# Laying k and v of five batches out the way q is laid out, and moving one transpose forward in the opening, in a fused linear-attention and SwiGLU kernel

## The chip, the cores and the metric

The kernel runs on one core of a Trainium2 chip. The metric is the device time of one execution in microseconds (us); lower is better. Every kernel is timed several times beside the unchanged kernel on the same chip. One early execution of the unchanged kernel took 857.58 us for no reason that was found. A profile is one execution recorded instruction by instruction. Its span is some 1.8 us shorter than the device time of the same execution (324.8 against 326.62 us for the kernel before), so spans are compared with spans and times with times.

The engines are called as in the profile: PE is the matrix engine (TensorE), PEld its weight loads, DVE the vector engine, ACT the scalar engine, POOL the GpSimd engine, SP the engine that issues most DMAs.

## The reference, cut to what matters

```python
# q, k, v: (8 batches, 8 heads, 576 tokens, 64) float32
theta = pi/2 * arange(576) / 576
phi(x) = concat([relu(x)*cos(theta), relu(x)*sin(theta)], axis=-1)   # 128 features
q_p, k_p = phi(q), phi(k)
kv  = einsum('bhsf,bhsd->bhfd', k_p, v)          # 128 x 64 per head, a sum over all 576 tokens
z   = sum(k_p, axis=2)
num = einsum('bhsf,bhfd->bhsd', q_p, kv)
den = einsum('bhsf,bhf->bhs', q_p, z) + 1e-6
x   = (num/den) as (4608 tokens, 512)
xn  = x / sqrt(mean(x*x) + 1e-6) * rms_g
out = (silu(xn @ w_gate) * (xn @ w_val)) @ w_out     # 512 -> 1536 -> 512, float32 out
```

The part that the change touches is kv and z. The kernel appends a column of ones to v (so E = 65 columns), and one matmul chain per head then gives kv and z together. This is called the kvz stage below: one for each batch, eight in all, and the change alters those of batches 3 to 7.

## The kernel before

Most of the time goes to the feed-forward part: blocks of 512 tokens, with 128x512 matmuls back to back. The attention of batch `nb` is slipped between the matmuls of block `nb-1`. 576 tokens are not a multiple of 128, so k and v are loaded with 9 tokens to a partition: two heads (2 x 576 tokens = 128 x 9) share the 128 partitions, the even head in rows 0 to 63 and the odd one in rows 64 to 127. So each matmul of the kvz stage uses 64 of the 128 rows, and it takes 8 heads x 9 = 72 of them.

```python
    def load_kv(which, b, r0=0, r1=4, j0=0, j1=NJ):          # NJ = 9
        ...  # raw tile [P, 4 pairs of heads, 9*64]
        return nc.sync.dma_start(
            out=raw[key][:, r0:r1, j0 * D : j1 * D],
            in_=src[b, 2 * r0 : 2 * r1, :, :].rearrange("h s d -> (h s d)")
            .rearrange("(r p n) -> p r n", p=P, n=NJ * D)[:, :, j0 * D : j1 * D],
        )

    def k_phi(eng, b, j, part, rs=(0, 4)):                    # one of the 9 tokens, cos or sin
        ...
        phi(eng, kp_main[b][:, j, rs[0] : rs[1], o],
            raw[("k", b)][:, rs[0] : rs[1], j * D : (j + 1) * D], f(5 + j))

    def kvz_mm(b, banks, rs=(0, 4)):
        for r in range(*rs):
            for j in range(NJ):
                for c in range(2):
                    lo = 64 * c
                    nc.tensor.matmul(
                        banks[c][:, r * E : (r + 1) * E],
                        lhsT=kp_main[b][lo : lo + 64, j, r, :],
                        rhs=vvm[b % 2][lo : lo + 64, r, j, :],
                        start=(j == 0), stop=(j == NJ - 1),
                    )
    # ... cut: q, whose tiles hold 4 tokens of a head to a partition (512 tokens, all 128 rows);
    # the last 64 tokens of heads 0-3 and 4-7 share a fifth tile (rows 0-63 and 64-127)

    # the opening, batch 0 (cut)
    q_tr_evac(A, 0, 2, psO[0][:, :])
    q_phi(A, 0, 3, 1)
    ...
    nd_pe(0, 2, psA)                    # products of q tile 2 with kvz
    nd_post(0, 2, psA)
    q_tr_pe(0, 3, psO[1][:, :])         # transposes of q tile 3
    q_tr_evac(A, 0, 3, psO[1][:, :])
    ...
    # loads of batches 3..7 run two batches ahead, one piece after each step of a block
```

Of the kernel before, what the change touches and what calls it, by code (L numbers as in the profile page):

```python
# [9 lines left out]
FP32 = mybir.dt.float32  # L10
BF16 = mybir.dt.bfloat16
AF = mybir.ActivationFunctionType
ALU = mybir.AluOpType
SYNC_DEP = mybir.DependencyInfo(mybir.DependencyClass.Sync, mybir.DependencyReason.DATA)



# [6 lines left out]
def kernel(  # L24
# [11 lines left out]
    nc = tc.nc  # L36
    B, H, S, D = q.shape
    DM = H * D
# [32 lines left out]
    def load_kv(which, b, r0=0, r1=4, j0=0, j1=NJ):  # L71

        key = (which, b)
        if key not in raw:
            raw[key] = (two if which == "k" else one).tile(
                [P, 4, NJ * D], FP32, name=f"r{which}", tag=f"r{which}"
            )
        src = {"k": k, "v": v}[which]
        return nc.sync.dma_start(
            out=raw[key][:, r0:r1, j0 * D : j1 * D],  # L80
            in_=src[b, 2 * r0 : 2 * r1, :, :]
            .rearrange("h s d -> (h s d)")
            .rearrange("(r p n) -> p r n", p=P, n=NJ * D)[:, :, j0 * D : j1 * D],
        )
# [10 lines left out]
    def load_q_tail(b):  # L95
# [6 lines left out]
            )  # L102
        return d

    def load_piece(which, b, p):
        if which != "q":
            load_kv(which, b, p, p + 1)
        elif p < 4:
            load_q(b, 2 * p, 2 * p + 2)
        else:  # L110
            load_q_tail(b)
# [68 lines left out]
    wg = one.tile([P, NDT, DFF], BF16, name="wg")  # L180
    wv = one.tile([P, NDT, DFF], BF16, name="wv")
    wo = one.tile([P, NNT, DM], BF16, name="wo")
    vvm = [one.tile([P, 4, NJ, E], BF16, name=f"vvm{i}") for i in range(2)]
    xnt_tail = one.tile([P, NDT, TB], BF16, name="xnt_tail")
    NXT = 5
    xts = [one.tile([P, DM + 4], FP32, name=f"xt{i}") for i in range(NXT)]
    for i in range(2):
        nc.gpsimd.memset(vvm[i][:, :, :, D:E], 1.0)
    eps_col = math.sqrt(DM * 1e-6)
    for i in range(NXT):  # L190
        nc.gpsimd.memset(xts[i][:, DM : DM + 1], eps_col)
# [16 lines left out]
    def phi(eng, out_ap, in_ap, scale):  # L208
        if eng is nc.scalar:
            nc.scalar.activation(out=out_ap, in_=in_ap, func=AF.Relu, scale=scale)  # L210
        else:
            eng.tensor_scalar(  # L212
                out=out_ap, in0=in_ap, scalar1=scale, scalar2=0.0, op0=ALU.mult, op1=ALU.max
            )

    def k_phi(eng, b, j, part, rs=(0, 4)):

        o = slice(0, D) if part == 0 else slice(D, F)
        f = cos_of if part == 0 else sin_of
        if b not in kp_main:  # L220
            kp_main[b] = one.tile([P, NJ, 4, F], BF16, name="kpm", tag="kpm")
        phi(
            eng, kp_main[b][:, j, rs[0] : rs[1], o],
            raw[("k", b)][:, rs[0] : rs[1], j * D : (j + 1) * D], f(5 + j),
        )

    def q_phi(eng, b, c, part):
        o = slice(0, D) if part == 0 else slice(D, F)
        f = cos_of if part == 0 else sin_of
        if (b, c) not in qp_tiles:  # L230
            qp_tiles[(b, c)] = four.tile(
                [P, H if c < 4 else 4, F], BF16, name="qp", tag="qp" if c < 4 else "qpt"
            )
        src = view4(raw[("q", b)], c) if c < 4 else raw[("qt", b)][:, :, :]
        phi(eng, qp_tiles[(b, c)][:, :, o], src, f(c))
# [15 lines left out]
    def q_tr_pe(b, c, bank):  # L251
        t = qp_tiles[(b, c)]
        dst = bank.bitcast(BF16).rearrange("p (h s) -> p h s", s=P)
        for h in range(H if c < 4 else 4):
            nc.tensor.transpose(dst[:, h, :], t[:, h, :], ident[:, :])  # L255

    def q_tr_evac(eng, b, c, bank, heads=(0, 8)):
        h0, h1 = heads if c < 4 else (0, 4)
        dst = bank.bitcast(BF16).rearrange("p (h s) -> p h s", s=P)
        copy(eng, q_dst(b, c)[:, h0:h1, :], dst[:, h0:h1, :])  # L260

    def copy(eng, o, i):
        if eng is nc.scalar:
            nc.scalar.copy(out=o, in_=i)  # L264
        else:
            eng.tensor_copy(out=o, in_=i)  # L266

    def v_cast(eng, b, r0=0, r1=4, j0=0, j1=NJ):
        copy(
            eng, vvm[b % 2][:, r0:r1, j0:j1, 0:D],  # L270
            raw[("v", b)][:, r0:r1, j0 * D : j1 * D].rearrange("p r (j d) -> p r j d", d=D),
        )

    def headview(pst):
        return pst[:, :, 0 : 4 * E].rearrange("p b (h e) -> p b h e", e=E)
# [29 lines left out]
    def nd_pe(b, j, pst):  # L305

        o = headview(pst)
        for h in range(H):
            g, i = h // 4, h % 4
            if j < 4:  # L310
                nc.tensor.matmul(  # L311
                    o[:, g, i, :], lhsT=qpT[(b, 0)][:, h, j * P : (j + 1) * P],
                    rhs=kvz_of(b, h), start=True, stop=True,
                )
            else:
                for bb in (b - 1, b):
                    lo = 64 * (bb % 2)
                    nc.tensor.matmul(
                        o[lo : lo + 64, g, i, :],
                        lhsT=qpT[(bb, 1)][:, i, 64 * g : 64 * g + 64],  # L320
                        rhs=kvz_of(bb, h), start=True, stop=True,
                    )
# [59 lines left out]
        rs_of[(b, j)] = rs  # L382

    xn_of = {}
    xg = one.tile([P, DM], FP32, name="xg")

    def x_gain(b, j, g):

# [41 lines left out]
    def x_tr_evac(eng, b, j, bank, part=(0, 4)):  # L430
        dst = bank.bitcast(BF16).rearrange("p (t s) -> p t s", s=P)
        copy(eng, x_dst(b, j)[:, part[0] : part[1], :], dst[:, part[0] : part[1], :])
# [167 lines left out]
    for half, (eng, bank) in enumerate(((A, psG[1]), (V, psV[1]))):  # L600
        part = (2 * half, 2 * half + 2)
        x_tr_pe(0, 0, bank[:, :], part)
        x_tr_evac(eng, 0, 0, bank[:, :], part)
    q_tr_evac(A, 0, 2, psO[0][:, :])
    q_phi(A, 0, 3, 1)
    x_norm(0, 1)
    q_phi(V, 0, 3, 0)
    open_ffn(0, (0, 1), 0, 128)
    x_tr_pe(0, 1, psV[1][:, :])
    x_tr_evac(V, 0, 1, psV[1][:, :])  # L610
    nd_pe(0, 2, psA)
    nd_post(0, 2, psA)
    q_tr_pe(0, 3, psO[1][:, :])
    q_tr_evac(A, 0, 3, psO[1][:, :])
    x_sq(0, 2)
    wo_load(0)
# [40 lines left out]
    def at(blk, n, where, f, *args):  # L657
        slots.setdefault((blk, n), none())[where].append((f, args))
# [26 lines left out]
    for nb in range(2, B):  # L685
        b = nb - 1
        late = nb == 2
        vb, vn = (b, 3) if late else (b - 1, 14)
        if nb == 3:
            vb, vn = b, 1  # L690
        if late:
            at(vb, vn, "post", v_cast, V, nb, *LOW)
        for j in range(NJ):
            kb, kn = (b, 1 + j // 7) if late else (b - 1, 12 + j // 3)
            if not late or j > 3:
                at(kb, kn, "post", k_phi, V, nb, j, 0)
            if not late or j > 1:
                at(kb, kn, "post", k_phi, A, nb, j, 1)
        for c in range(5):
            qn = (2, 3, 5, 5, 6)[c] if late else c  # L700
            at(b, qn, "post", q_phi, V, nb, c, 0)
            at(b, qn, "post", q_phi, A, nb, c, 1)
            at(b, qn, "post", q_tr_dma, nb, c)
        if not late:
            at(vb, vn, "post", v_cast, V, nb, *LOW)
        at(vb, vn + 1, "post", v_cast, V, nb, *HIGH)
        kz, nds = (6, (7, 9, 11, 12)) if late else (4, (5, 7, 9, 11))
        at(b, kz, "pe", kvz_pe, nb, psA)
        at(b, kz, "pre", kvz_evac, A, nb, psA, 0)
        at(b, kz, "pre", kvz_evac, A, nb, psA, 1)  # L710
        for j in range(4):
            n = nds[j]
            at(b, n, "mid" if n == NNT else "pe", nd_pe, nb, j, psA)
            at(b, n, "pre", nd_post, nb, j, psA)
            at(b, n, "post", x_sq, nb, j)
            where = "pre" if n + 1 >= NNT else "post"
            at(b, n + 1, where, x_norm, nb, j)
            at(b, n + 1, where, x_tr_dma, nb, j)
        if nb % 2 == 1:
            at(b, 13, "pe", nd_pe, nb, 4, psA)  # L720
            at(b, 13, "pre", nd_post, nb, 4, psA)
            at(b, 13, "post", x_sq, nb, 4)
            at(b, 14, "post", x_norm, nb, 4)
            at(b, 14, "post", x_tr_dma, nb, 4)
    for nb in range(3, B):

        b = nb - 2
        for i, which in enumerate(("k", "v", "q")):
            if (which, nb) == ("v", 3):
                at(b, 13, "post", load_kv, "v", nb, *LOW)  # L730
                at(b, 14, "post", load_kv, "v", nb, *HIGH)
                continue
            for p in range(5 if which == "q" else 4):
                n = (0, None, 6)[i] + p if b == 1 else 5 * i + p
                at(b + n // 16, n % 16, "post", load_piece, which, nb, p)

# [157 lines left out]
```

## Time and profile before

| what | value |
|---|---|
| time, median of 3 | 327.7 us (327.57, 327.7 and the one of 857.58, which is counted) |
| profiled execution | 326.62 us, span 324.8 us |
| PE busy | 316.5 us, 97% |
| matmuls of 512 columns, start to start | 216 ns |
| the five kvz stages, from the start of the matmul ahead to that of the one after | 1.58 us each |

Lines of the profile's page, kernel before: the span, busy time of each engine, the clock granted to PE in 40 slices (9 is 90% or more), the DMA packets, and the chain of waits that ended last by engine.

```profile
span 324.8 us, 6415 instructions
PE 316.5 (97%) x2409; PEld 161.8 (50%) x2444; DVE 186.0 (57%) x414; ACT 176.8 (54%) x367; POOL 31.9 (10%) x67
...
PEclk9999999999999999999999999999999999999999
...
DMA packets 80321, 53.91 MB, mean 166 GB/s; under 512 B 51361, under 2 KB 67745, under 8 KB 80290
...
PE 91%; ACT 4%; DVE 2%; issue 1%; DMA 1%; DVEq 0%; ACTq 0%
```

PE is the limit: it is busy nearly always and is 91% of the chain. Work taken from DVE or ACT is worth nothing unless PE waited for it.

One kvz stage in the timeline of PE, kernel before. The columns are start (us), duration (us), engine, line, operation, output and inputs, rows and columns, count:

```profile
96.17 1.03 PE L442 MATMUL psV<-xnT,wv 128*128 128x512 bf16 x4
97.13 1.33 PE L283 MATMUL psA<-vvm,kpm 64*128 64x65 bf16 x72
98.40 1.04 PE L442 MATMUL psG<-xnT,wg 128*128 128x512 bf16 x3
```

The same stage in the timeline of the weight loads, kernel before; in brackets stands the idle time ahead:

```profile
97.13 1.21 PEld L283 LDWEIGHTS <-kpm 64*128 64x128 bf16 x72 [0.42 <-issue]
```

Read the starts. Four matmuls of 512 columns begin at 96.17; the fourth should begin 3 x 216 ns later, at 96.82, and the next one 216 ns after that, at 97.03. The kvz stage begins at 97.13 instead. Its 72 matmuls run to 98.40, where the feed-forward goes on. In the start records behind these lines the last 512-column matmul takes 312 ns to the next start (96 more than its 216), and the last of the 72 takes 122 ns, where about 17 is usual for this form (105 more). The weight loads show the same edge: ahead of the first there is 0.42 us without a weight load, put down to nothing that the profile shows. So a stage costs 96 + 1143 + 122 = 1361 ns.

The groups of DVE and ACT that the change alters, kernel before (columns: line, engine, operation, output<-inputs, shapes, count | busy us, mean ns of one | idle before):

```profile
L210 ACT ACTIVATE kpm<-rk,tab 128x256 bf16<-128x256 f32 x63 | 27.4, 499 | 0.0
...
L212 DVE TENSOR_SCALAR kpm<-rk,tab 128x256 bf16<-128x256 f32 x63 | 18.1, 348 | 0.0
...
L311 PE MATMUL psA<-kvzs,qpT 128*128 128x65 bf16 x248 | 12.8, 194 | 0.3
...
L266 DVE CAST vvm<-rv 128x1152 bf16<-128x1152 f32 x13 | 9.5, 754 | 0.0
```

The PE line is not altered. It is the existing matmul of the form that the new kvz stage will have, 128 rows and 65 columns: eight of them start within 213 ns, so one every 30.5 ns. (The 194 ns is the latency of one, which overlaps with the next.)

The last lines that matter are those of the end: the last piece of the chain of waits, and then the closing instructions of SP (count, then min/median/max duration in ns, first and last start).

```profile
321.14 0.37 ACT osb L264
```

```profile
L889 SPq EVENT_SEMAPHORE  x11: 17/28/28, 322.1 to 324.8; - x11
...
L889 SPq DRAIN  x3: 7/7/13, 324.0 to 324.3; - x3
```

### The profile page before, as it was taken

Reading aid. Unit: us, or ns where it says so; the run is one execution under the profiler, and the core shown is the slowest. Engines: PE = TensorE matmul, PEld = TensorE weight load, DVE = VectorE, ACT = ScalarE, POOL = GpSimd, SP = SyncE. Lnnn points to the kernel's source line nnn. Section 1 sums busy time; section 2 is a strip of 40 time slices with the busy share of each in tenths; the row PEclk is TensorE's granted clock in tenths of the full one; section 3 lists DMA queues with packets and bytes.
Section 4 is the critical chain, followed back from the end, with each engine's and each line's share of the span. In section 5 each row is a group of like instructions: output and inputs, shape, how many; then the busy total and the mean of one; then the engine's idle time right before and its main releaser. Section 6 shows DMA issues by size and latency. Waiting matters only on the chain.

```text
span 324.8 us, 6415 instructions
## 1 busy us (share of the span) xinstructions
PE 316.5 (97%) x2409; PEld 161.8 (50%) x2444; DVE 186.0 (57%) x414; ACT 176.8 (54%) x367; POOL 31.9 (10%) x67
## 2 busy tenths in 40 slices
PE   8899999999999999999999999999999999999995
PEld 2587465554445444544454445444544444444443
DVE  6975768777766765578257745773577133203410
ACT  6973865965774467546664475456644233223321
POOL 1660202001100110010001100110011000000000
PEclk9999999999999999999999999999999999999999
DMA  7999999797599576976597679956611400020014
GB/s 258 274 199 251 313 200 337 270 193 195 141 276 265 159 195 164 211 195 192 160 212 211 165 195 218 199 151 214 126 39 32 131 32 0 26 105 1 0 34 97
DMA packets 80321, 53.91 MB, mean 166 GB/s; under 512 B 51361, under 2 KB 67745, under 8 KB 80290
## 3 DMA queue, kind: packets, MB, share of 16 engines
q1 hardware_dynamic: 73248, 48.64, 57.6%
q0 software_dynamic: 6880, 4.72, 9.9%
q8 instruction: 19, 0.31, 0.4%
q10 hardware_dynamic: 162, 0.13, 0.2%
q14 instruction: 12, 0.10, 0.1%
HBM read 37.75 MB, written 9.44 MB: 145 GB/s over the span
## 4 chain that ended last, share of the span: by engine, by line
PE 91%; ACT 4%; DVE 2%; issue 1%; DMA 1%; DVEq 0%; ACTq 0%
PE psC L462 26%; PE psG L442 26%; PE psV L442 26%; PE psA L283 3%; PE psA L311 2%; ACT kpm L210 2%; PE psG L462 2%; PE psG L581 1%; DMA rk<-in_k_dram 1%; PE psV L581 1%; PE psO L581 1%; PE psV L255 1%; ACT qp L210 1%; PE psO L255 1%; ACT sg L451 0%
## 5 line engine op out<-in xcount | busy, mean ns | idle before, releaser
L457 DVE TENSOR_TENSOR hT<-psV,sg 128x512 bf16<-128x512 f32 x102 | 70.3, 689 | 93.9 <-PE psV L442 70.1
L451 ACT ACTIVATE sg<-psG 128x512 f32<-128x512 f32 x102 | 60.6, 594 | 65.1 <-PE psG L442 63.9
L442 PE MATMUL psV<-xnT,wv 128*128 128x512 bf16 (+1 forms) x365 | 92.1, 374 | 0.4
L442 PE MATMUL psG<-xnT,wg 128*128 128x512 bf16 (+1 forms) x352 | 90.9, 374 | 0.7
L462 PE MATMUL psC<-wo,hT 128*128 128x512 bf16 x382 | 88.2, 379 | 0.7
L442 PEld LDWEIGHTS <-wv 128*128 128x128 bf16 x416 | 40.7, 98 | 47.4
L462 PEld LDWEIGHTS <-hT 128*128 128x128 bf16 x420 | 40.2, 98 | 46.7
L442 PEld LDWEIGHTS <-wg 128*128 128x128 bf16 x416 | 38.5, 98 | 41.0 <-DVE xnT L266 0.4
L264 ACT COPY osb<-psC 128x512 f32<-128x512 f32 (+1 forms) x33 | 19.1, 578 | 39.7 <-PE psC L462 39.0
L381 POOL TENSOR_TENSOR rs<-ms,mhalf 128x1 f32<-128x1 f32 x36 | 19.8, 549 | 199.8 <-ACT scr L376 199.8
L403 DVE SCALAR_TENSOR_TENSOR xn<-xt,rs,gb 128x512 bf16<-128x512 f32 x35 | 26.1, 745 | 16.6 <-POOL rs L381 16.6
L376 ACT ACTIVATE scr<-xt 128x513 bf16<-128x513 f32 x36 | 22.8, 635 | 22.8 <-DVE xt L365 22.6
L210 ACT ACTIVATE kpm<-rk,tab 128x256 bf16<-128x256 f32 (+1 forms) x78 | 31.9, 477 | 1.6 <-DMA rk<-in_k_dram 1.6
L365 DVE TENSOR_TENSOR xt<-psA,rec 128x512 f32<-128x512 f32 x35 | 24.2, 691 | 1.2
L212 DVE TENSOR_SCALAR kpm<-rk,tab 128x256 bf16<-128x256 f32 (+1 forms) x84 | 22.3, 330 | 2.1 <-DMA rk<-in_k_dram 2.1
L210 ACT ACTIVATE qp<-rq,tab 128x512 bf16<-128x512 f32 x32 | 22.4, 714 | 0.0
L212 DVE TENSOR_SCALAR qp<-rq,tab 128x512 bf16<-128x512 f32 x32 | 15.1, 485 | 0.0
L311 PEld LDWEIGHTS <-qpT 128*128 128x128 bf16 x248 | 11.6, 98 | 6.7 <-issue 0.3
L311 PE MATMUL psA<-kvzs,qpT 128*128 128x65 bf16 x248 | 12.8, 194 | 0.3
L442 PE MATMUL psG<-xnt_tail,wg 128*128 128x512 bf16 x48 | 12.3, 379 | 0.1
L442 PE MATMUL psV<-xnt_tail,wv 128*128 128x512 bf16 x47 | 12.1, 379 | 0.0
L283 PEld LDWEIGHTS <-kpm 64*128 64x128 bf16 x576 | 9.9, 94 | 3.5 <-issue 2.7
(91 smaller groups left out, 170.3 us busy)
## 6 DMA issues: line engine op xcount, KB each, us to landing
out_dram<-osb SPq DMA_DIRECT2D x32, 256.0 KB, 2.8
rk<-in_k_dram SPq DMA_DIRECT2D x21, 288.0 KB, 4.6
rq<-in_q_dram SPq DMA_DIRECT2D x20, 256.0 KB, 3.1
rv<-in_v_dram SPq DMA_DIRECT2D x17, 288.0 KB, 3.2
rv<-in_v_dram SPq DMA_DIRECT2D x5, 576.0 KB, 7.7
rq<-in_q_dram SPq DMA_DIRECT2D x2, 1024.0 KB, 8.7
wo<-in_moe_w_out_dram POOLq DMA_DIRECT2D x4, 384.0 KB, 6.9
rk<-in_k_dram SPq DMA_DIRECT2D x2, 576.0 KB, 4.1
```

The source lines that it names most:

```text
L210: nc.scalar.activation(out=out_ap, in_=in_ap, func=AF.Relu, scale=scale)
L212: eng.tensor_scalar(out=out_ap, in0=in_ap, scalar1=scale, scalar2=0.0, op0=ALU.mult, op1=ALU.max)
L283: nc.tensor.matmul(banks[c][:, r * E : (r + 1) * E], lhsT=kp_main[b][lo : lo + 64, j, r, :], rhs=vvm[b % 2][lo : lo + 64, r, j, :], start= ...
L311: nc.tensor.matmul(o[:, g, i, :], lhsT=qpT[(b, 0)][:, h, j * P : (j + 1) * P], rhs=kvz_of(b, h), start=True, stop=True,)
L365: nc.vector.tensor_tensor(out=xt[:, 0:DM].rearrange("p (b h d) -> p b h d", b=2, d=D), in0=o[:, :, :, 0:D], in1=rec[:, :, :].unsqueeze(3). ...
L376: nc.scalar.activation(out=scr[:, :], in_=xt[:, 0 : DM + 1], func=AF.Square, scale=1.0 / math.sqrt(DM), accum_out=ms[:, :],)
L381: nc.gpsimd.tensor_tensor(out=rs[:, :], in0=ms[:, :], in1=mhalf[:, :], op=ALU.pow)
L403: nc.vector.scalar_tensor_tensor(out=xn[:, :], in0=x_of[(b, j)][:, 0:DM], scalar=rs_of[(b, j)][:, :], in1=gb[:, :], op0=ALU.mult, op1=ALU. ...
L442: nc.tensor.matmul(pst[bank][:, cols[0] : cols[1]], lhsT=w[:, t, n * P : (n + 1) * P], rhs=x[:, t, cols[0] : cols[1]], start=(t == 0), sto ...
L451: nc.scalar.activation(out=sg[:, :], in_=psG[bank][:, :], func=AF.Silu)
L457: nc.vector.tensor_tensor(out=hTs[blk][:, n, :], in0=psV[bank][:, :], in1=sg[:, :], op=ALU.mult)
L462: nc.tensor.matmul(bank, lhsT=hTs[blk][:, n, j * P : (j + 1) * P], rhs=wo[:, n, :], start=(n == 0), stop=(n == NNT - 1),)
```

## The change

Its intent: k and v of batches 3 to 7 take q's layout. A partition holds 4 tokens of every head, so 512 tokens fill all 128 rows and give 4 matmuls per head. The last 64 tokens of heads 0 to 3 lie in rows 0 to 63 of a fifth tile, those of heads 4 to 7 in rows 64 to 127. The fifth matmul of a head uses all 128 rows too, against a v tile `vvt` that is zero in the other heads' rows, so it stays in the same mode of the array. A stage has 40 matmuls in place of 72, and five wide phi operations for each of cos and sin in place of nine narrow ones. In the opening, q tile 3 is transposed ahead of tile 2's products.

```diff
+    def load_heads(which, b, h0, h1):
+        nc.sync.dma_start(
+            out=kv_tile(which, b)[:, h0 * 4 * D : h1 * 4 * D].rearrange("p (h n) -> p h n", n=4 * D),
+            in_=src[b, h0:h1, 0:512, :].rearrange("h (p j) d -> p h (j d)", j=4))
+    def load_last(which, b):                     # two DMAs: heads 0-3, heads 4-7
+        for g in range(2):
+            nc.sync.dma_start(
+                out=kv_tile(which, b)[64 * g : 64 * g + 64, 2048:2304]...,
+                in_=src[b, 4 * g : 4 * g + 4, 512:576, :].rearrange("h s d -> s h d"))
...
+    vvt = [one.tile([P, H, E], BF16, name=f"vvt{i}") for i in range(2)]
     for i in range(2):
         nc.gpsimd.memset(vvm[i][:, :, :, D:E], 1.0)
+        nc.gpsimd.memset(vvt[i][64:128, 0:4, :], 0.0)
+        nc.gpsimd.memset(vvt[i][0:64, 4:8, :], 0.0)
+        nc.gpsimd.memset(vvt[i][0:64, 0:4, D:E], 1.0)
+        nc.gpsimd.memset(vvt[i][64:128, 4:8, D:E], 1.0)
...   (k_phi_as_q: 5 operations of 512, the fifth of 256; v_cast_as_q on DVE;
...    v_cast_last: two casts of 64x256 on POOL)
+    def kvz_as_q(b, pst):
+        for h in range(H):
+            for c in range(5):
+                nc.tensor.matmul(
+                    pst[:, h % 2, h // 2 * E : (h // 2 + 1) * E],
+                    lhsT=kp_of(b)[:, 8 * c + (h if c < 4 else h % 4), :],
+                    rhs=vv_of(b)[:, c, h, :] if c < 4 else vvt[b % 2][:, h, :],
+                    start=(c == 0), stop=(c == 4))
...   (a scratch tile shares the buffers of another, to make room for vvt)
+    q_phi(A, 0, 3, 1)
     q_tr_evac(A, 0, 2, psO[0][:, :])
-    q_phi(A, 0, 3, 1)
...
+    q_tr_pe(0, 3, psO[1][:, :])
     nd_pe(0, 2, psA)
     nd_post(0, 2, psA)
-    q_tr_pe(0, 3, psO[1][:, :])
...
-        at(b, kz, "pe", kvz_pe, nb, psA)
+        at(b, kz, "pe", kvz_pe if late else kvz_as_q, nb, psA)       # late: batch 2
...
-            for p in range(5 if which == "q" else 4):
+            for p in range(5):                                       # 6 DMAs for k, 6 for v
```

## The prediction

> **What bounds the kernel.** TensorE. PE is busy 316.5 of 324.8 us (97%, page), granted clock 1.00 (DVE 57%, ACT 54%, POOL 10%); the chain of waits is 91% PE. In order of time, full matmuls (128x512) start every 216 ns nearly without holes from 30 us on. A block is 33.4 to 33.9 us: 144 of them (31.1 us), its products with kvz, one kvz stage. So only PE time or a new PE wait counts.
>
> **PE, the five kvz stages of batches 3 to 7.** Before: 72 matmuls with 64 rows, in pairs, 1143 ns from first to last start. The last 512-column matmul ahead of them takes 312 ns to the next start (216 is normal), the last of the 72 122 ns (17 is normal). The Trainium skill, "TensorEngine Tiling (Array Packing)", Key Properties, says that changing the tiling mode drains TensorE; these 96 and 105 ns agree. In all 96+1143+122 = 1361 ns. After: 40 matmuls of 128x128 weights and 65 columns, no change of mode. The products with kvz have the same form and start every 30.5 ns (213 ns over 7), so 40 x 30.5 = 1220 ns. Gain 0.14 us a stage, 0.7 us in all, on the chain.
>
> **DVE and ACT.** k of a batch: nine operations of 256 elements (348 ns on DVE, 499 on ACT) become four of 512 (485 and 714, as q's) and one of 256: -0.85 us DVE, -1.14 us ACT a batch. v's casts: 1152 to 1024 elements, 754 to some 680 ns. About -5 us on each engine, off the chain: worth nothing.
>
> **POOL.** Eight memsets at the start (free: weight loads wait 8.1 us there anyway) and two casts of 64x256 a batch, estimated 0.4 to 0.7 us each from the 0.55 us of one-element work in the trace.
>
> **DMA.** k and v of a batch go from 512 runs of 2304 B each to 1024 of 1 KB and 512 of 256 B: some 10,000 more packets, and 20 more issues of about 0.6 us on SP. DMA is 60 to 70% busy and loads come early, so this is hidden, but for v of batch 3. Before, its second half landed at 95.6 us and kvz started at 97.1. Now its last tokens land later (estimate 96 to 96.5), then come two POOL casts in turn; kvz needs the first at its fifth matmul. I expect one PE wait of 0 to 0.6 us, some 0.2.
>
> **Opening.** Before, PE waits 0.18 us for q tile 3's phi after tile 2's products. Now the transposes go first, but the products wait for an eviction that ACT does after the phi (0.74+1.02 us, to about 18.9). PE waits as long elsewhere. Worth 0, at most 0.1 either way.
>
> **Sum.** 327.7 - 0.7 + 0.2 + 0.0 = 327.2 us; range 326.3 to 328.2. Faster by over 2%: 0.01; within 2%: 0.97; slower: 0.02.
>
> **What would show it.** Right: the five kvz stages show 40 matmuls about 30 ns apart, no 312 and 122 ns at their edges, blocks of batches 4 to 7 shorter by about 0.14 us; DVE about 181 us, ACT about 171; the opening ends as before. Wrong: kvz matmuls further apart than 30 ns, a PE wait on POOL's vvt longer than 0.6 us or in more than one block, q transposes of batch 3 (2 us of slack) late behind SP's extra issues. Another risk: k or v of later blocks late, a us or more each.

## The result, and the profile after

The changed kernel takes 327.03 us (median of 6, 326.72 to 327.26), the kernel before 327.5 us beside it. The ratio of the two is 0.999, with a 95% interval of 0.9976 to 1.0004: the same, by a threshold of 2%. Ratios here are the mean time of one kernel's fast runs over that of the other's of the same rounds, so they are not quite the ratio of the medians. The difference of those means is 0.33 us (327.36 to 327.03). Executions over 1.5% slower than the fastest of the same kernel are left out of the means.

The same lines of the page, kernel after:

```profile
span 325.4 us, 6119 instructions
PE 316.4 (97%) x2249; PEld 162.6 (50%) x2284; DVE 183.9 (57%) x394; ACT 173.4 (53%) x347; POOL 38.9 (12%) x85
...
PEclk9999999999999999999999999999999999999999
...
DMA packets 90881, 53.90 MB, mean 166 GB/s; under 512 B 56801, under 2 KB 83425, under 8 KB 90850
...
PE 90%; DMA 3%; ACT 2%; DVE 2%; issue 1%; SPq 0%; DVEq 0%
```

The span is longer by 0.6 us although the times are shorter. One profiled execution is one draw: the start of this one happened to be late, as is shown below. So the two traces are compared part by part, not by their totals.

The kvz stage in the timeline of PE, kernel after:

```profile
97.05 1.03 PE L524 MATMUL psV<-xnT,wv 128*128 128x512 bf16 x4
97.91 0.29 PE L349 MATMUL psA<-vvm,kpm 128*128 128x65 bf16 x4
98.03 0.19 PE L349 MATMUL psA<-vvt,kpm 128*128 128x65 bf16 x1
98.06 0.29 PE L349 MATMUL psA<-vvm,kpm 128*128 128x65 bf16 x4
...
99.10 0.20 PE L349 MATMUL psA<-vvt,kpm 128*128 128x65 bf16 x1
99.13 0.81 PE L524 MATMUL psG<-xnT,wg 128*128 128x512 bf16 x2
```

Its weight loads, kernel after:

```profile
97.70 1.47 PEld L349 LDWEIGHTS <-kpm 128*128 128x128 bf16 x40
```

Both edges are gone. The first kvz matmul starts at 97.91, four times 216 ns after 97.05, and the feed-forward goes on 0.03 us after the last kvz matmul. The weight loads begin 0.2 us ahead of their matmuls, with no idle time noted: they overlap with the matmuls before, which they did not across the old edge. In the start records: 216 ns in, 1183 to 1185 ns from first to last start, 34 or 35 ns out, so 1219 ns where the prediction said 1220.

The groups of DVE, ACT and POOL, kernel after:

```profile
L247 ACT ACTIVATE kpm<-rk,tab 128x512 bf16<-128x512 f32 x20 | 13.3, 714 | 0.0
...
L249 DVE TENSOR_SCALAR kpm<-rk,tab 128x512 bf16<-128x512 f32 x20 | 8.9, 492 | 0.0
...
L318 DVE CAST vvm<-rv 128x1024 bf16<-128x1024 f32 x10 | 6.5, 681 | 0.0
...
L318 POOL CAST vvt<-rv 64x256 bf16<-64x256 f32 x10 | 5.4, 536 | 6.1 <-DMA rv<-in_v_dram 5.8
```

The end, kernel after: the last piece of the chain, then the closing instructions of SP.

```profile
321.25 0.37 ACT osb L316
```

```profile
L978 SPq EVENT_SEMAPHORE  x11: 17/28/28, 322.2 to 325.4; - x11
...
L978 SPq DRAIN  x3: 7/7/41, 324.6 to 324.9; - x3
```

Here is something that nobody had planned. From the start of the last ACT copy to SP's first closing DRAIN it was 324.0 - 321.14 = 2.86 us; now it is 324.6 - 321.25 = 3.35 us. The last stores are the same ones. Half a microsecond is lost after all work is done.

Three parts of the span can be told apart in the start records of PE. They are the same from one profile to the next where the code is the same, but for the first:

| profile of | start to first kvz matmul | kvz of batch 1 to last matmul | last matmul to end |
|---|---|---|---|
| before | 10.70 | 277.34 | 4.00 |
| after | 11.61 | 276.58 | 4.51 |
| e1 before again | 10.93 | 277.35 | 4.00 |
| e2 layout only | 10.77 | 276.59 | 4.53 |
| e3 opening only | 10.88 | 277.36 | 4.01 |
| e4 memsets late | 11.87 | 276.60 | 4.51 |
| e9 four DMAs fewer | 10.81 | 276.58 | 4.25 |
| e10 eight DMAs fewer | 10.63 | 276.58 | 4.08 |
| e11 before, four DMAs more | 10.76 | 277.35 | 4.07 |
| e12 batches 1 to 7 | 10.76 | 276.11 | 4.10 |

(The stretch that is left out, first kvz matmul to kvz of batch 1, is 32.79 to 32.80 us with the old opening and 32.74 to 32.76 with the new one; 32.65 in e12.) The middle part is 0.76 us shorter with the new layout, and the end 0.51 us longer. The first part varies by over 1 us, whatever the kernel.

### The profile page after: what moved, and what is told of

Read it like the earlier page. It is cut to its first block, busy times and chain, and to the rows that moved or that the text cites. A ratio compares the mean times of both kernels' runs of the same rounds, so it can differ in the third digit from the quotient of the medians.

```text
span 325.4 us, 6119 instructions
## 1 busy us (share of the span) xinstructions
PE 316.4 (97%) x2249; PEld 162.6 (50%) x2284; DVE 183.9 (57%) x394; ACT 173.4 (53%) x347; POOL 38.9 (12%) x85
## 2 busy tenths in 40 slices
DMA packets 90881, 53.90 MB, mean 166 GB/s; under 512 B 56801, under 2 KB 83425, under 8 KB 90850
## 4 chain that ended last, share of the span: by engine, by line
PE 90%; DMA 3%; ACT 2%; DVE 2%; issue 1%; SPq 0%; DVEq 0%
PE psC L544 26%; PE psV L524 26%; PE psG L524 26%; DMA rv<-in_v_dram 3%; PE psA L393 2%; PE psA L349 2%; PE psG L544 2%; PE psG L663 1%; PE psV L663 1%; PE psO L663 1%; PE psA L365 1%; ACT kpm L247 1%; PE psV L307 1%; ACT sg L533 0%; PE psA L400 0%
## 5 line engine op out<-in xcount | busy, mean ns | idle before, releaser
L247 ACT ACTIVATE kpm<-rk,tab 128x256 bf16<-128x256 f32 (+2 forms) x58 | 28.2, 545 | 1.7 <-DMA rk<-in_k_dram 1.7
L249 DVE TENSOR_SCALAR kpm<-rk,tab 128x128 bf16<-128x128 f32 (+2 forms) x64 | 20.2, 374 | 2.3 <-DMA rk<-in_k_dram 2.3
L318 DVE CAST vvm<-rv 128x1024 bf16<-128x1024 f32 (+4 forms) x16 | 10.3, 670 | 0.2 <-DMA rv<-in_v_dram 0.2
```

Of the source, the lines that this page charges most:

```text
L247: nc.scalar.activation(out=out_ap, in_=in_ap, func=AF.Relu, scale=scale)
L249: eng.tensor_scalar(out=out_ap, in0=in_ap, scalar1=scale, scalar2=0.0, op0=ALU.mult, op1=ALU.max)
```

## The experiments

Twelve kernels ran. The questions were: is the shorter stage really the two changes of mode, or only the fewer matmuls; what does the opening do, and why was the start late; and where does the half microsecond at the end come from.

### e1: the kernel before, once more

No edit; it tells how far two runs of one kernel differ.

> The kernel before, unchanged, as a control. Theory 1: the first loads land at times that differ from run to run, and the 0.9 us by which the changed kernel's opening is later in its profile (first q landed at 9.34 instead of 8.43 us, first kvz matmul at 11.61 instead of 10.70 us) is such a difference. Then this profile may have its first kvz matmul anywhere from 10.6 to 11.7 us, and its time against the same kernel has a ratio of 1.000 with an interval about 0.001 wide. Rival: the change delays the first loads. Then the first kvz matmul stands at 10.7 us here, within 0.1 us. Either way the five kvz stages take 1.36 us each.

Measured: 326.91 us against 326.88, ratio 1.0001 (0.9988 to 1.0013). Times of a kernel spread over 0.6 to 0.8 us from run to run here (1.9 us for the kernel before beside e9), and with five runs the interval is 0.13% to each side, 0.4 us. The differences that this study looks for are of that size, so the parts of the profile must carry the argument.

### e2, e3, e4: each half of the change alone, and the memsets moved

Three theories for the late start in the profile after (11.61 us to the first kvz matmul, 10.70 before): the first loads land at other times from run to run, whatever the kernel; the new order of the opening; the eight new memsets on POOL, which run at 1.95 to 4.04 us.

e2 is the kernel after with the old order of the opening:

```diff
-    q_phi(A, 0, 3, 1)
     q_tr_evac(A, 0, 2, psO[0][:, :])
+    q_phi(A, 0, 3, 1)
...
-    q_tr_pe(0, 3, psO[1][:, :])
     nd_pe(0, 2, psA)
     nd_post(0, 2, psA)
+    q_tr_pe(0, 3, psO[1][:, :])
```

> The changed kernel with the opening's order put back, so the layout of k and v alone. Theory: the layout gives 0.14 us in each of five kvz stages and nothing else on TensorE, so 0.7 us or a ratio of 0.998, and the five stages take 1.22 us each; the stretch from the first kvz matmul to the first 512-column matmul is as long as in the kernel before (18.85 us). Rival: the opening's new order gives part of the gain, then this run gains less than the changed kernel by that part.

Measured: 326.70 us against 326.88, ratio 0.9996 (0.9982 to 1.0009).

e3 is the kernel before with the new order, the same edit the other way round:

```diff
+    q_phi(A, 0, 3, 1)
     q_tr_evac(A, 0, 2, psO[0][:, :])
-    q_phi(A, 0, 3, 1)
...
+    q_tr_pe(0, 3, psO[1][:, :])
     nd_pe(0, 2, psA)
     nd_post(0, 2, psA)
-    q_tr_pe(0, 3, psO[1][:, :])
```

> The kernel before with the opening's new order alone. Theory: a PE wait of 0.18 us goes and waits of about the same size come in its place, so from the first kvz matmul to the first 512-column matmul it takes 18.85 us as before, within 0.1 us, and the time is the same (ratio 0.9995 to 1.0005). Rival: q tile 3 ahead of tile 2's products shortens the opening by 0.2 us or more. The five kvz stages stay at 1.36 us.

Measured: 327.16 us against 326.88, ratio 1.0006 (0.9993 to 1.0018).

e4 is the kernel after with the new memsets late:

```diff
         nc.gpsimd.memset(vvm[i][:, :, :, D:E], 1.0)
-        nc.gpsimd.memset(vvt[i][64:128, 0:4, :], 0.0)     # and the three others
...
     wo_load(3)
+    for i in range(2):
+        nc.gpsimd.memset(vvt[i][64:128, 0:4, :], 0.0)     # and the three others
```

> The changed kernel with the eight POOL memsets of the padding tiles moved from the start to after the weight loads. Rival of theory 1: the 2.3 us of memsets at the start delay the first loads or the first operations on DVE by 0.1 to 0.9 us; then this kernel is faster than the changed one by that much, its first kvz matmul at 10.7 us. Theory 1 (run to run): first kvz matmul anywhere from 10.6 to 11.7 us, time as the changed kernel's within 0.3 us.

Measured: 327.32 us against 326.88, ratio 1.0006 (0.9994 to 1.0019).

No time tells these apart, but the table above does. The middle part has two values, 277.34 to 277.36 with the old layout and 276.58 to 276.60 with the new one, and the order of the opening does not touch it. The order is worth 0.05 us, in the stretch ahead of batch 1's kvz: 32.79 to 32.80 us in every profile with the old order, and 32.74 to 32.76 in every one with the new order and batch 1 in the old layout. And the memsets are not the cause of a late start: the latest start of all, 11.87 us, was e4's, which has no new memset there.

What the start follows is the first loads. In 14 profiles the first kvz matmul came at 10.63 to 11.87 us, after the first q load landed at 8.18 to 9.61 and the first v load at 9.69 to 11.12. In the profile after they landed at 9.34 and 10.86, in that of before at 8.43 and 9.94. Its chain of waits starts with that load (columns: start, us, what):

```profile
2.27 8.59 DMA rv<-in_v_dram
```

This is the "DMA 3%" in the page's chain after. It is no cost of the new layout; v of batch 0 is loaded as before.

The timelines of PE show why the new order is worth little. Kernel before, with the transposes (psO) behind the products (psA):

```profile
18.05 0.39 PE L428 MATMUL psV<-ident,xn 128*128 128x128 bf16 x4
18.27 0.41 PE L311 MATMUL psA<-kvzs,qpT 128*128 128x65 bf16 x8
18.70 0.62 PE L255 MATMUL psO<-ident,qp 128*128 128x128 bf16 x8
19.15 0.39 PE L581 MATMUL psG<-xnT,wg 128*128 128x128 bf16 x4
```

Kernel after (0.91 us later in all, because of the late start):

```profile
18.96 0.39 PE L510 MATMUL psV<-ident,xn 128*128 128x128 bf16 x4
19.28 0.61 PE L307 MATMUL psO<-ident,qp 128*128 128x128 bf16 x8
19.73 0.41 PE L393 MATMUL psA<-kvzs,qpT 128*128 128x65 bf16 x8
19.97 0.39 PE L663 MATMUL psG<-xnT,wg 128*128 128x128 bf16 x4
```

From the first of these lines to the last it is 1.10 us before and 1.01 after, and of that 0.05 us is left by the kvz stage of batch 1: the wait has moved from between products and transposes (18.27 to 18.70 for eight products that need 0.24) to ahead of the transposes (18.96 to 19.28 for work of 0.22). Most of it stays.

### e5 and e6: the change of mode put back in measured amounts

Theory: the gain of a stage is the drain at a change of the array's mode; the 40 matmuls themselves are no faster than the 72. Rival: the gain comes from having fewer matmuls, and the edges are only a form of it. To tell them apart, the fifth matmul of each head is made to use only the 64 rows that hold its tokens (the zero padding is then not read). The count stays 40, the results stay right, but the mode changes. In e5 each head's half matmul stands alone, so a stage has eight visits to the half-row mode; in e6 two heads share one, so it has four.

```diff
+    def kvz_one(b, pst, h, c):
+        g, i = h // 4, h % 4
+        rows = slice(0, P) if c < 4 else slice(64 * g, 64 * g + 64)
+        nc.tensor.matmul(
+            pst[:, g, i * E : (i + 1) * E],
+            lhsT=kp_of(b)[rows, 8 * c + (h if c < 4 else i), :],
+            rhs=vv_of(b)[:, c, h, :] if c < 4 else vvt[b % 2][rows, h, :],
+            start=(c == 0), stop=(c == 4))
     def kvz_as_q(b, pst):
-        ... (40 matmuls of 128 rows)
+        for h in range(H):                    # e5
+            for c in range(5):
+                kvz_one(b, pst, h, c)
+        for i in range(4):                    # e6 instead
+            for h in (i, 4 + i):
+                for c in range(4):
+                    kvz_one(b, pst, h, c)
+            for h in (i, 4 + i):
+                kvz_one(b, pst, h, 4)
```

(Heads 0 to 3 now sit in one bank of PSUM and 4 to 7 in the other.)

> The changed kernel with the zero padding not used: the fifth matmul of each head takes only the 64 rows that hold its tokens, so TensorE changes between 128 and 64 rows and back 8 times in a kvz stage (heads 0 to 3 in one bank, 4 to 7 in the other, so that the two halves never meet in a bank). Theory (the change of row tiling costs about 96 ns going in and 105 ns coming out, whatever stands around it): each such matmul costs 127+122 ns where two starts took 61, so +0.19 us a head, +1.5 us a stage, and +7.5 us in all against the changed kernel: about 334.5 us. Rival (the gain comes from fewer and larger matmuls, and what shows at the edges is only the end of the 512-column matmuls): the same 40 matmuls take 1.2 us as before, 327 us in all.

Measured: 335.07 us against 327.0, ratio 1.0247 (1.0232 to 1.0262), slower. The timeline of PE in e5:

```profile
132.71 0.29 PE L349 MATMUL psA<-vvm,kpm 128*128 128x65 bf16 x4
132.93 0.20 PE L349 MATMUL psA<-vvt,kpm 64*128 64x65 bf16 x1
133.06 0.30 PE L349 MATMUL psA<-vvm,kpm 128*128 128x65 bf16 x4
133.29 0.20 PE L349 MATMUL psA<-vvt,kpm 64*128 64x65 bf16 x1
```

A head takes 0.35 to 0.36 us here, where it took 0.15 in the kernel after. In the start records, the lone half matmul comes 124 ns after the full one ahead of it, and the next full one 132 ns later. A stage is 2744 + 134 ns against 1185 + 34, 1.66 us more, so 207 ns for each visit. Beyond the usual 30.5 ns the two edges are 93 and 101 ns, close to the 96 and 105 of the kernel before.

> As the run with 64 rows at each head, but two heads of different halves are done together, their two 64-row matmuls next to each other: 4 changes of tiling in and out per stage in place of 8. Theory: 127+16+122 ns where 91 stood, so +0.17 us a pair, +0.7 us a stage, +3.5 us in all: about 330.5 us. Rival (not the changes of tiling): 327 us.

Measured: 330.91 us against 327.0, ratio 1.0120 (1.0103 to 1.0138): the same by the threshold of 2%, but clear of the noise. A stage takes 1800 + 133 ns, 0.71 us more for four visits, 178 ns each. One stage of the five took 2094 from first to last start: in this order heads 4 to 7 are wanted early, and its chain of waits shows PE held by v's second cast until 97.90 us.

What follows: at an unchanged number of matmuls, the stage grows nearly in step with the number of mode changes (1.66 us for eight visits, 0.71 for four), by an amount that a visit's two edges of the kernel before (96 + 105 = 201 ns) foretell. The edges explain the whole gain. Indeed they are more than all of it: without them, 72 matmuls at 16.1 ns take 1.16 us and 40 at 30.5 ns take 1.22. The new matmul stream is 0.06 us longer than the old one, and the edges that it saves are 0.20 us.

### e7 and e8: the kvz stages four times over

The same question from the other side: repeat the stage's matmuls four times inside one visit, in the old form (e7) and in the new one (e8). The edges then stay as they are while the stream is quadrupled. The chain of each head starts anew each time, so results stay right.

```diff
     def kvz_pe(b, pst):                                        # e7, from the kernel before
-        kvz_mm(b, [pst[:, c, :] for c in range(2)])
+        for _ in range(4 if b >= 3 else 1):
+            kvz_mm(b, [pst[:, c, :] for c in range(2)])

     def kvz_as_q(b, pst):                                      # e8, from the kernel after
-        for h in range(H):
+        for h in [h for _ in range(4) for h in range(H)]:
```

> The kernel before with each of the five kvz stages of batches 3 to 7 done four times in a row (same result). Theory: 72 matmuls take 72 x 16.1 = 1.16 us and the changes at the edges, 0.20 us, come once however often the stage is repeated; so +3 x 1.16 x 5 = +17.4 us over the kernel before.

Measured: 357.81 us against 327.0, ratio 1.0943 (1.0909 to 1.0976): 30.8 us more, where 17.4 was expected. This is a miss.

> The changed kernel with each of its five kvz stages done four times in a row. Theory: 40 matmuls take 40 x 30.5 = 1.22 us with nothing at the edges, so +3 x 1.22 x 5 = +18.3 us over the changed kernel; the changed layout's advantage of 0.7 us turns into a loss of about 0.2 us against the kernel before repeated likewise. Rival (40 matmuls are simply less work than 72): the advantage grows to 4 x 0.7 = 2.8 us.

Measured: 344.65 us against 327.0, ratio 1.0540 (1.0525 to 1.0556): 17.65 us more than the kernel before. The 18.3 us that were expected are over the kernel after, which was not timed again beside this run. In the trace a stage of 160 matmuls takes 4834 + 34 ns, four times 1.22 us, and the five stages together are 18.3 us longer than those of the kernel after, as expected.

The miss of e7 lies in one hole in each long stage. A piece of its chain of waits:

```profile
97.50 3.77 PE psA L283 x227
101.28 1.98 issue
103.26 1.88 PE psA L283 x61
105.14 0.54 PE psG L443
```

Up to the hole the matmuls start every 16.1 ns, as they do before; then PE stands for 2.17 us (from start to start) with nothing to wait for that the profile shows. The five holes are 2.17, 2.00, 2.76, 2.37 and 1.51 us long and come after 178 to 258 matmuls, that is after 356 to 516 instructions of PE, weight loads counted. Each lies at a DMA of the kind "instruction" of 16 KB: for the first, 100.79 to 101.97 us. All five holes end 1.3 to 1.5 us after such a DMA does. So I infer, but no run shows it directly, that PE had used up its instructions and waited for the next ones. In e8 instructions are used at half that rate (one per 15 ns, against one per 8 ns), and there is no hole in 320 of them.

The first hole cost twice. Stretches of e7, with busy time and count of PE, PEld, DVE, ACT and POOL, then the granted clock, DMA share and GB/s:

```profile
97.50:101.28 3.78, 3.78 (x228) 3.65 (x227) 1.20 (x3) 0.38 (x1) 0.00 (x0) 1.00 1.18 283
...
103.26:105.20 1.94, 1.94 (x62) 1.84 (x63) 0.00 (x0) 0.02 (x1) 0.00 (x0) 0.50 0.78 228
```

After it the clock was 0.50 for 3.41 us, and the rest of the matmuls ran at half speed. The other four holes did not lower it. The Trainium skill, "TensorE: Matmul & The Clock Gate", Part 1, says that the clock falls to half after an idle window of about 3.4 us; here a hole of 2.17 us was enough once, while one of 2.76 us was not. The duration of the slow spell fits the page's window. A look at the clock records explains more: in all 14 traces every stretch at one clock, but for the last, lasts a whole multiple of 3.413 us (in e7 29, 1 and 73 times). Laid on these steps, the first hole has 2.08 us in a single one, and the others at most 1.54. So it may be the idle part of a step that counts, and not the length of the hole; one fall does not prove that.

What follows: the five holes come to 10.8 of the 13.4 us that were not expected; the slow spell to about 1.4, an estimate (0.67 us inside the stage, and half of the 1.5 us that it lasted after it); some 1.2 us is not traced. As a comparison of the two forms in time, the pair is spoiled. Inside the unbroken stretches it agrees with e5 and e6: without edges the old form is not the slower one. And it shows a second thing against short half-row matmuls: a long run of them outpaces something that a run of full ones does not.

### e9, e10, e11: what makes the end longer

SP ends the kernel by waiting for eight DMA semaphores one after another, in a fixed order of semaphores, and then draining. DMAs take the semaphores in turn, so another number of DMAs puts the last store on another semaphore. Two theories. Theory L: it matters which semaphores of that fixed order the last stores hold, and the order in the kernel after makes one of the waits slow. Theory F: the 24 more instructions of SP (343 against 319) push a closing instruction to a place in its program where the next one is slow to come, whatever it is. (These counts are of the built program. Two of its instructions are branches, which leave no record, so a trace has 341 against 317.) Times at which the eight waits and the drain end, in us from the start of the last matmul, out of the records of SP:

```
        wait 1  wait 2  wait 3  wait 4  wait 5  wait 6  wait 7  wait 8  drain   SP instructions
before  2.708   2.770   2.834   2.896   2.955   3.017   3.076   3.138   3.188   319
after   1.312   1.625   1.819   2.972   3.042   3.112   3.182   3.575   3.677   343
e9      2.708   2.769   2.834   2.895   2.954   3.015   3.075   3.165   3.214   339
e10     1.313   1.595   1.813   2.973   3.033   3.094   3.153   3.215   3.259   335
e11     1.312   1.647   1.818   2.960   3.019   3.081   3.140   3.202   3.252   323
```

In the kernel after, wait 8 takes 0.39 us, from 3.18 to 3.57, though its own DMA landed at 0.56 us and the last store at 2.93 us, as in the kernel before (2.92). Removing four DMAs keeps the long program but puts the semaphores back in the order of before; removing eight does the same for the place in the program, with the semaphores as in after; adding four to the kernel before changes the order alone.

e9 loads k and v of batch 7, and e10 those of batches 6 and 7, in two pieces of four heads instead of four of two:

```diff
+                if nb in (7,) and which != "q" and p < 4:          # e10: nb in (6, 7)
+                    if p % 2 == 0:
+                        at(b + n // 16, n % 16, "post", load_heads, which, nb, 2 * p, 2 * p + 4)
+                    continue
                 at(b + n // 16, n % 16, "post", load_piece, which, nb, p)
```

> The changed kernel with k and v of batch 7 loaded in two pieces of four heads each in place of four of two: 4 DMAs fewer on SP. In all profiles so far the stretch from the last matmul's start to the end is 4.0 us with the old layout and 4.5 us with the new one, and it holds SP's closing waits for the eight DMA semaphores, taken in a fixed order; the DMAs go round these eight, 20 more of them shift the last ones by four places, and one wait (semaphores 110 and 109) takes 0.39 us where others take 0.06 to 0.07. Theory L (which semaphore the last stores use): with 16 more DMAs the last stores use the same semaphores as in the kernel before, so the end takes 4.0 us and the time is 0.5 us below the changed kernel's. Rival F (the length of SP's program: the slow wait stands where the next piece of it has to come): 4 instructions fewer move the slow place 4 instructions later, past the waits, and the end takes 4.3 to 4.5 us.

Measured: 326.07 us against 326.99, ratio 0.9978 (0.9957 to 0.9999); last matmul to end 4.25 us.

> As the run with four DMAs fewer, but k and v of batches 6 and 7: 8 DMAs fewer than in the changed kernel. Theory L: the last stores use the same semaphores as in the changed kernel, so the end takes 4.5 us as there, with the slow wait at semaphores 110 and 109. Rival F: the slow place moves 8 instructions later and out of the closing waits, so the end takes about 4.1 us (the order of the waits alone costs about 0.1).

Measured: 325.9 us against 326.99, ratio 0.9971 (0.9954 to 0.9989); last matmul to end 4.08 us.

e11 is the kernel before, with k and v of batch 7 in four DMAs more:

```diff
+                if nb == 7 and which != "q" and p < 2:
+                    for j0, j1 in ((0, 5), (5, NJ)):
+                        at(b + n // 16, n % 16, "post", load_kv, which, nb, p, p + 1, j0, j1)
+                    continue
```

> The kernel before with 4 DMAs more on SP (the first two pieces of k and of v of batch 7 each cut in two). Theory L: the last stores use the semaphores that they use in the changed kernel, so the end takes 4.5 us in place of 4.0. Rival F: SP's program is 323 instructions long, between 319 and 343, no slow wait, and the end takes 4.0 to 4.15 us. The kvz stages stay at 1.36 us.

Measured: 326.75 us against 326.99, ratio 0.9993 (0.9973 to 1.0014); last matmul to end 4.07 us.

Theory L falls: e11 and e10 have the semaphore order of after, and the end is 4.07 and 4.08 us, 0.07 or 0.08 more than before and not 0.5. Theory F stands, and e9 shows it best. There the eight waits are nearly as quick as before (wait 8 takes 0.09 us), but the slow instruction has not gone away; it has moved to a later DRAIN. The closing DRAINs of SP, e9:

```profile
L982 SPq DRAIN  x3: 7/7/130, 323.4 to 324.0; - x3
```

And e10, where it is gone:

```profile
L982 SPq DRAIN  x3: 7/7/7, 323.2 to 323.5; - x3
```

Counted along SP's program, wait 8 of the kernel after and the slow DRAIN of e9 are both its instruction number 338; the kernels whose program ends before that place (before, e10, e11, and e12 with 337 instructions) have no slow one. That a place and not an instruction is slow is shown. The records hold more for it: in all 14 traces SP's 80th and 208th records, and in the seven that are long enough its 336th (the program's 338th), come at least 365 ns after the one before them has ended, whatever they are. Ahead of the 80th it is 443 to 467 ns, whether that is a load or a wait. Apart from the 13th, which waits for weights, and the very last, no other place is late in every trace. So the place comes back every 128 instructions; it costs nothing where SP has time. Why it is slow is not shown. An 8 KB DMA of the kind "instruction" runs near it, but in the kernel after it starts at 4.18 us, 0.60 us after wait 8 has ended, so it is not what that wait waited for. That the supply of SP's program is behind it is an inference.

### e12: the new layout for batches 1 and 2 too, with fewer DMAs

If the edges and the end are all there is, a kernel with more stages converted and a shorter SP program must beat both. e12 puts k and v of batches 1 and 2 into q's layout as well, and loads k and v of batches 4 to 7 in two large pieces each (337 SP instructions).

```diff
-    load_kv("k", 1, 0, 1)
+    load_heads("k", 1, 0, 2)
...  (the other loads, phis and casts of batches 1 and 2 likewise)
-        at(b, kz, "pe", kvz_pe if late else kvz_as_q, nb, psA)
+        at(b, kz, "pe", kvz_as_q, nb, psA)
...
+                if nb in (4, 5, 6, 7) and which != "q" and p < 4:     # as in e9
```

> A version that should beat both: the changed kernel with k and v of batches 1 and 2 in q's layout too, and k and v of batches 4 to 7 loaded in two pieces each, so that SP's program is 337 instructions long (the slow place found so far is the 338th). Theory: the kvz stages of batches 1 and 2 also lose the two changes of tiling, 0.14 us each, so seven stages of 1.22 us; the end takes 4.0 to 4.1 us; together 0.7 + 0.28 + 0.05 - 0.05 = 1.0 us below the kernel before, ratio 0.997. What could take it back: the casts of batch 1's or 2's last tokens on POOL or the later landing of batch 1's k in the busy opening make TensorE wait before these two stages.

Measured: 326.01 us (325.4 to 326.44) against 326.97, ratio 0.9971 (0.9951 to 0.9990), correct. In the profile, first kvz matmul to the end is 308.76 + 4.10 us, against 310.14 + 4.00 before, so 1.28 us less. The stages of batches 1 and 2 also take 1183 + 34 ns, and a wait of 0.24 us in batch 2's stage for v's second cast is gone. By its ratio it is level with e10, which ran on another chip: the start's jitter is as large as what is between them. Nor does the time show that e12 beats the kernel after, since the two intervals overlap; its parts do, 312.86 us against 313.83 from the first kvz matmul to the end. Both e10 and e12 are faster than the kernel before by about 0.3%, with intervals that leave 1.0 out, and that is still far below the 2% that would count as faster.

## Why the prediction was right, and where its sum was not

The predicted time (327.2) and class (the same) held: 327.03 us. Point by point:

- **PE is the limit, and only its time counts.** Right. DVE and ACT lost 2.1 and 3.4 us of busy time, and only the PE part of the table moved.
- **kvz stages, -0.7 us.** Right, in size and cause. A stage went from 1361 to 1219 ns (predicted 1220), 0.71 us in five. The part of the profile that holds them is 0.76 us shorter; the last 0.05 us is not traced. From one kvz stage to the next it is 0.15 us less, where 0.14 was predicted. The Trainium skill, "TensorEngine Tiling (Array Packing)", Key Properties, states that changing the tiling mode drains TensorE; the trace agrees, with 96 and 105 ns at the edges, and e5 and e6 confirm that the cost comes with the changes, by putting them back (207 and 178 ns for each visit).
- **Opening, 0.0.** It is -0.05 us, inside the 0.1 that was allowed.
- **A PE wait on v of batch 3, +0.2 us.** Mis-sized: it is 0. The last of v landed at about 96.5 us, at the late end of the estimate, but the two POOL casts took 0.39 and 0.40 us, at 96.60 and 97.05, and the matmul that needs the first one started at 98.03 in an undisturbed stream. In the other profiles with the new layout but e4 the first cast ended 0.65 to 1.6 us ahead of its use. In e4 the casts ended only 0.24 and 0.05 us ahead of their use, so such a wait is near; that stage was 15 ns longer.
- **The end of the kernel.** No term for it stood in the sum, and it cost +0.5 us. This is the step that the prediction had wrong: "20 more issues of about 0.6 us on SP ... this is hidden" counted what the issues delay and not that the program gets longer. It got 24 instructions longer, and its 338th, which is slow, then fell into the closing waits that everything depends on (e9, e10). Of the 0.51 us some 0.08 is the new order of the semaphores alone (e10, e11); the rest is that place.
- **DVE about 181 us, ACT about 171 us.** Mis-sized: 183.9 and 173.4. The durations of single operations were right (714 ns for ACT's 512, 492 against a predicted 485 for DVE's, 681 against 680 for the cast), and the durations of k's and v's operations, added up, fell by 4.5 and 5.7 us. But busy time fell by only 2.1 and 3.4. Operations that follow one another overlap in the records, by about 83 ns on DVE and 99 on ACT, and with fewer operations 1.8 and 2.3 us of such overlap went; on DVE some 0.6 us more was lost because other operations took longer. Fewer, longer operations save less than their mean durations say.
- **Some 10,000 more packets, hidden.** Right: 80321 to 90881, and no new wait of PE on a load.

So the sum was -0.7 + 0.2 + 0.0 = -0.5 and the parts measured are -0.76 + 0.0 - 0.05 + 0.51 = -0.30; the times differ by -0.33. The total was near partly by luck: the wait that did not come, and the somewhat larger gain, made up for over half of the cost that was not foreseen. Luck is in the starting value too: 327.7 is a median that counts the 857.58, and from the mean of its fast runs, 327.36, the same sum gives 326.86. The ratio's interval holds 1.0, so the time alone shows no gain; what is shown of the change is in the parts.

## What to carry to other kernels

Where a busy matrix engine passes from full-row to half-row matmuls and back, look at the start-to-start times at the edges and not at busy time: here each visit cost some 0.2 us, so a few zero-padded rows were cheaper than the mode that would have skipped them. When a change adds DMAs, count also what it adds to the program of the engine that issues them, and read the closing waits at the very end of the trace, where nothing hides a delay. And when two executions differ by a few tenths of a microsecond, cut the traces into parts that repeat exactly before believing either total.

## What the Trainium skill lacked or had wrong

- "TensorEngine Tiling (Array Packing)" says that a change of mode drains TensorE, but gives no cost. Here: 96 ns into and 105 ns out of a run of 64-row matmuls beyond their usual spacing, and 124 + 132 ns from start to start around a lone one.
- "TensorE: Matmul & The Clock Gate", Back-to-back issue gap, gives N/2.4 + 2.5 ns for the gap of a lone matmul (for 65 columns an estimate of 29.6 ns from it), and says that a stream with a weight load per matmul runs slower at small N (81 ns for N = 128) and faster at large N (131 ns for N = 512). Here such streams keep to the formula: 30.5 ns for 65 columns, 216 ns for 512.
- The same page, Part 1, ties the fall to half clock to an idle window of about 3.4 us. In e7 it fell after a hole of 2.17 us, for 3.41 us, and did not fall after four others of 1.51 to 2.76 us. So a wholly idle window was not needed: 2.08 us of one step of 3.413 us were idle when it fell, and at most 1.54 us when it did not.
- "Runtime: NRT & Kernel Launch", Instruction fetch mechanics, treats how an engine's instructions are supplied, but gives no measured stall in straight code. In e7 there are five holes of 1.5 to 2.8 us after 356 to 516 instructions at 8 ns each, at an instruction DMA of 16 KB each time; none in e8 at 15 ns. That the supply of instructions is the cause is inferred.
- Neither that section nor another page tells of slow places in SP's program every 128 instructions: the 338th took 0.39 us as a wait that was long met, and as a DRAIN it came 0.39 us late and took 0.13 us, where others take 7 to 44 ns; the 80th and 208th records come at least 0.37 us late in all 14 traces.
- "GPSIMD Engine Reference", Specifications, says that GpSimd shares SBUF interfaces with VectorE, with contention for DVE instructions in a 2-port mode or with two SBUF inputs, but gives no amount there ("SBUF — State Buffer" treats the sharing at more length). The two lines below, of the timeline of DVE in the kernel after, are the same operation without and with POOL's casts (96.60 to 97.45 us) beside it. Over all profiles, 128x512 phi operations that overlapped a POOL cast took 558 to 672 ns, but for five at 469 to 479, the duration without one; casts of 1024 took 872 to 896 instead of 675 to 693, but for one at 689; the product that reads PSUM stayed at 676 to 693. It is off the critical path here.

```profile
95.34 0.48 DVE L249 TENSOR_SCALAR qp<-rq,tab 128x512 bf16<-128x512 f32 x1
...
97.06 0.67 DVE L249 TENSOR_SCALAR qp<-rq,tab 128x512 bf16<-128x512 f32 x1
```
